# Joining values products with later scores on TensorE, and a retuned order of work, in an attention and mixture-of-experts kernel

## The chip, the cores and the metric

The kernel runs on one core of one Trainium2 chip. The metric is the device time of one execution in microseconds (us), the median of several runs; less is better.

## The reference

Attention with two kinds of mask feeds a dense mixture of experts. The shapes are batch 4, 8 heads, sequence 576, head width 64; then 2304 rows of 512, 4 experts, inner width 1024, all in float32.

```python
scores = scale * np.matmul(q, k.transpose(0, 1, 3, 2))
mask_local = (rel >= 0) & (rel < stride)          # heads 0 to 3, stride 32
mask_strided = (rel >= 0) & (pos[None, :] % stride == pos[:, None] % stride)   # heads 4 to 7
scores = np.where(masks[None, :, :, :], scores, -1000000000.0)
attn = softmax(scores)                            # max, exp, sum + 1e-9, divide
x = np.matmul(attn, v)                            # heads side by side: 2304 x 512
...
p = domain_probs / (domain_probs.sum(-1, keepdims=True) + 1e-09)
for e in range(E):
    h = np.maximum(x @ w1[e], 0.0)
    out += p[:, e:e + 1] * (h @ w2[e])
```

## The kernel before, in words

**Attention.** The work is cut into 16 pairs of two heads each, in the order of the batches, and within a batch local, strided, local, strided (`KORD`). `plan_pair(n)` records the steps of pair n: the loads of q, k and v on SP's queue; the scores on TensorE (L627 for local, L616 for strided heads) into the PSUM tag `sc`; the masking out of PSUM on DVE (L641); the maximum (L644), its subtraction (L647), exp on ACT (L651), the sum (L655) and the division (L659); the transposes on TensorE (L706, L722, L739) into `ps`; their copies `pT` (L526, L528); the values product on TensorE (L771, for the first batch's local heads L791) into `ps`; and the copies of the result into `x` as a high and a low part (`xh` L849, `xl` L852) or as it is (`xr`). PSUM has four banks `mo`, two `sc` and two `ps` (`BANKS`).

**Experts.** There are eight units (an expert and half of its inner width). For the first 384 rows each unit takes a plain first product (L969, 48 matmuls of 384 columns) and a plain second one (L985, 36 matmuls of 512 columns), each with operands split into a high and a low part (ACT L884, then VectorE or GpSimd L885). These run from about 18 to 197 us, with the attention of the later pairs between them. The other 1920 rows follow in two parts, by a scheme with fewer block products (L1155, twelve matmuls to a pair of block products), whose operands come back from DRAM (`ring`, `a`, `s`) and whose sums go out through `acc`. The very last product is cut into two halves of 256 columns in `plan_o`; two additions (L1338) and two stores (L1340) follow.

**What sets the order.** `Plan` records every step as an operation with an engine, a duration, the names it reads and writes, and a priority (a due time, corrected by the table `SHIFT`). `walk` plays the engines forward and takes, for each engine that is free, the operation that is ready and due first; on TensorE attention and experts take turns by a credit. The result is a fixed list of instructions for each engine, which the engine runs in order. An operation on TensorE is never split: all its matmuls follow each other. In the first 30 us `fill` puts dummy matmuls of 512 columns (L1526, into a free bank) where TensorE would stand idle; at most `FIRST` of them may stand ahead of the first real work. Whoever waits is held up in its place, and so is all behind it on its engine.

```python
add("PE", 1.05 if kd == "L" else 0.88, pv, ...pT, vst..., oks, zg[0] + 7, oks, cols=1092)
...
nc.vector.tensor_reduce(out=psums, in_=prs, op=ALU.add, axis=AX.X)
nc.vector.tensor_scalar_add(out=psums, in0=psums, scalar1=1e-9)      # L1464
```

## Time and profile before

| | |
|---|---|
| median of 3 runs | 778.45 us (776.25 to 778.79) |
| the profiled execution: its time | 778.49 us |
| its span, first to last instruction | 776.7 us |
| PE, TensorE matmul: busy | 765.5 us, 99% of the span |
| DVE, ACT, POOL: busy | 80%, 50%, 27% of the span |

The page divides the span into shares; a timeline row says when an instruction or a merged group of them began and how long it took, and in brackets how long its engine had stood idle before it and what ended that. Matmuls overlap, so the step between two of them is read from their starts. [...] A matmul in plain float32 is two instructions in the trace for each one in the program, with a weight load each.

### The profile page before, as it was taken

How to read it: one execution, taken by the hardware profiler on the slowest of the kernel's cores; microseconds unless marked ns; L12 is line 12 of the kernel's file. 1: busy time of each engine (PE TensorE's matmuls, PEld its weight loads, DVE VectorE, ACT ScalarE, POOL GpSimd, SP SyncE). 2: the span in 40 equal slices, each digit the busy share in tenths (PEclk: the TensorE clock that was granted, in tenths of full speed). 3: DMA queues.
4: the chain of work that ended last, by engine and by line, in shares of the span. 5: the costliest groups of instructions: out<-in, count | busy, mean ns of one | idle time of the engine just before them, and what ended most of it. 6: DMA issues, size and time to landing. Idle time of an engine off the chain costs nothing.

```text
span 776.7 us, 14119 instructions
## 1 busy us (share of the span) xinstructions
PE 765.5 (99%) x5374; PEld 664.6 (86%) x5377; DVE 620.8 (80%) x1016; ACT 385.6 (50%) x726; POOL 206.4 (27%) x198
## 2 busy tenths in 40 slices
PE   7999999999999999999999999999999999999997
PEld 4788888889989999999999998888888888888886
DVE  6877777798698897889798997758765976599895
ACT  4635544474566375646727654644354344523330
POOL 5412011012131522454373264001000330033250
PEclk9999999999999999999999999999999999999999
DMA  9999999778899798899989838955665697659624
GB/s 321 305 394 380 339 326 353 276 252 327 311 388 343 257 359 288 328 237 350 350 254 275 272 119 221 395 207 220 236 265 198 193 215 288 232 173 247 215 82 162
DMA packets 89630, 212.67 MB, mean 274 GB/s; under 512 B 7071, under 2 KB 33883, under 8 KB 89563
## 3 DMA queue, kind: packets, MB, share of 16 engines
q1 hardware_dynamic: 83659, 201.96, 71.8%
q0 software_dynamic: 5760, 9.70, 7.9%
q8 instruction: 42, 0.69, 0.3%
q10 hardware_dynamic: 144, 0.11, 0.1%
q14 instruction: 25, 0.20, 0.1%
HBM read 138.58 MB, written 73.17 MB: 273 GB/s over the span
## 4 chain that ended last, share of the span: by engine, by line
PE 95%; DVE 2%; DMA 1%; ACT 1%; issue 1%; POOL 0%; DVEq 0%; ACTq 0%
PE mo L1155 26%; PE ps L1155 25%; PE sc L1155 20%; PE mo L985 9%; PE mo L969 9%; PE ps L771 2%; DMA ring<-d27a 1%; PE sc L627 1%; PE ps L739 1%; PE sc L616 1%; PE mo L1526 1%; PE ps L791 0%; ACT q L1207 0%; DVE w2t L885 0%; DVE pmL L641 0%
## 5 line engine op out<-in xcount | busy, mean ns | idle before, releaser
L1155 PE MATMUL sc<-T,ring 128*128 128x448 f32 (+2 forms) x774 | 174.3, 374 | 0.0
L1155 PEld LDWEIGHTS sc<-T,ring 128*128 128x128 f32 x774 | 144.5, 188 | 19.7
L1240 ACT ACTIVATE T<-q 128x512 fp32r<-128x512 f32 (+1 forms) x196 | 112.6, 601 | 69.0 <-PE mo L1155 26.4
L1242 DVE TENSOR_TENSOR T<-q,T 128x512 fp32r<-128x512 f32 (+1 forms) x152 | 104.7, 703 | 15.9 <-ACT T L1240 15.2
L1203 DVE TENSOR_TENSOR q<-ps,v 128x448 f32<-128x448 f32 (+1 forms) x96 | 62.5, 654 | 35.3 <-PE ps L1155 30.9
L1155 PE MATMUL mo<-T,ring 128*128 128x512 f32 (+1 forms) x396 | 90.0, 376 | 0.0
L1207 ACT ACTIVATE q<-q 128x448 f32<-128x448 f32 (+1 forms) x84 | 49.9, 598 | 71.7 <-DVE q L1203 70.8
L1155 PEld LDWEIGHTS mo<-T,ring 128*128 128x128 f32 x396 | 74.3, 188 | 10.3
L1242 POOL TENSOR_TENSOR T<-q,T 128x448 fp32r<-128x448 f32 (+1 forms) x44 | 53.1, 1215 | 91.8 <-ACT T L1240 69.9
L985 PE MATMUL mo<-w2t,hs 128*128 128x512 f32 x288 | 71.2, 397 | 0.0
L1194 ACT ACTIVATE v<-mo 128x448 f32<-128x448 f32 (+1 forms) x96 | 54.5, 567 | 25.7 <-PE mo L1155 25.0
L1352 DVE TENSOR_TENSOR acc<-sc,acc 128x512 f32<-128x512 f32 (+1 forms) x85 | 54.9, 654 | 13.9 <-PE sc L1155 13.1
L1284 POOL TENSOR_TENSOR q<-q,q 128x512 f32<-128x512 f32 (+1 forms) x12 | 15.4, 1284 | 181.5 <-DVE T L1242 164.9
L985 PEld LDWEIGHTS mo<-w2t,hs 128*128 128x128 f32 x288 | 52.7, 188 | 11.0
L1284 DVE TENSOR_TENSOR q<-q,q 128x448 f32<-128x448 f32 (+1 forms) x88 | 58.9, 681 | 2.5 <-POOL T L1242 1.4
L526 ACT ACTIVATE acc<-sc 128x448 f32<-128x448 f32 (+1 forms) x41 | 23.2, 567 | 48.5 <-PE sc L1155 46.9
L969 PE MATMUL mo<-xh,a 128*128 128x384 f32 x192 | 45.7, 341 | 0.0
L1352 DVE TENSOR_TENSOR acc<-mo,acc 128x512 f32<-128x512 f32 (+1 forms) x52 | 34.0, 658 | 14.0 <-PE mo L1155 11.3
L1155 PE MATMUL ps<-T,ring 128*128 128x448 f32 (+1 forms) x180 | 40.8, 375 | 0.5 <-DMA ring<-d27a 0.5
L1155 PEld LDWEIGHTS ps<-T,ring 128*128 128x128 f32 x180 | 33.7, 188 | 5.3 <-DVE acc L1352 0.8
L1155 PE MATMUL ps<-t4h,a 128*128 128x448 f32 (+1 forms) x128 | 35.2, 376 | 0.2 <-DVE q L1203 0.2
L1155 PE MATMUL ps<-t3h,s 128*128 128x448 f32 (+1 forms) x128 | 35.2, 376 | 0.1
(179 smaller groups left out, 1437.6 us busy)
## 6 DMA issues: line engine op xcount, KB each, us to landing
raw<-in_w SPq DMA_DIRECT2D x28, 1024.0 KB, 8.3
qkS<-in_qk_strided SPq DMA_DIRECT2D x16, 329.0 KB, 8.2
vstL<-in_v_local SPq DMA_DIRECT2D x6, 640.0 KB, 9.7
po<-acc POOLq DMA_DIRECT2D x16, 224.0 KB, 7.2
vstS<-in_v_strided SPq DMA_DIRECT2D x8, 384.0 KB, 7.8
a<-d16a SPq DMA_DIRECT2D x6, 512.0 KB, 8.7
ring<-d27a SPq DMA_DIRECT2D x6, 512.0 KB, 6.5
a<-d10a SPq DMA_DIRECT2D x6, 512.0 KB, 4.7
```

What stands on the lines that cost most here:

```text
L526: nc.scalar.activation(out=dst(), in_=src(held[key]), func=AF.Copy)
L771: nc.tensor.matmul(oo[hf][64 * h:64 * h + 64, o:o + w], a, pt[r, x, c0:c0 + w], start=True, stop=True)
L969: nc.tensor.matmul(pt[:, 0:TA], w[:, c % 2, (f % 2) * P:(f % 2) * P + P], (xl if i == 1 else xh)[c], start=j == 0, stop=j == 11)
L985: nc.tensor.matmul(pt, ht[f][:, ts], wt[f][:, cs], start=j == 0, stop=j == 11)
L1155: nc.tensor.matmul(pt, a[i == 2][:, j, f * P:f * P + P], skewed(b[i == 1][j], TH)[:, cs], start=bool(first) and n == 0, stop=True, skip_gr ...
L1194: add("ACT", TH / 1200 + 0.18, lambda: nc.scalar.activation(out=late["u"][i][:, 0:TH], in_=held[key][:, 0:TH], func=AF.Copy), [key, "late2 ...
L1203: add("DVE", DD, lambda: nc.vector.tensor_tensor(out=q(), in0=src(), in1=late["u"][i][:, 0:TH], op=ALU.add), [key, f"u{i}", "late2"], [tok ...
L1207: add("ACT", TH / 1200 + 0.2, lambda: nc.scalar.activation(out=q(), in_=q(), func=AF.Relu), ["late2"], [tok], zs)
L1240: add("ACT", TH / 1200 + 0.17, lambda src=src, hi=hi: nc.scalar.activation(out=hi(), in_=src(), func=AF.Copy), [tok, "late2"], [f"T{i}h{j} ...
L1242: add("VP", vp, lambda e, src=src, hi=hi, lo=lo: engine(e).tensor_tensor(out=lo(), in0=src(), in1=hi().bitcast(F32), op=ALU.subtract), [to ...
L1284: add("VP", vp, lambda e, d=d, x=x, y=y: engine(e).tensor_tensor(out=d[0](), in0=x[0](), in1=y[0](), op=ALU.subtract), [x[1], y[1]], [d[1] ...
L1352: add("DVE", DD, lambda av=av, key=key: nc.vector.tensor_tensor(out=av(), in0=held[key][:, 0:TH], in1=av(), op=ALU.add), [key], tok, zd)
```

## The change

From the sixth pair on (pairs 6 to 15, `JOINED`) the scores are no operation of their own: `plan_pair` became a generator that hands its scores to the pair two before it, whose values product and these scores are now one operation on TensorE, with the names and banks of both. After an attention operation the planner keeps to attention while one is ready within 0.2 us (`STAY`). Twelve dummy matmuls of 64 columns (`PAD`) follow the scores of pair 1, at most six dummies precede the first scores (`FIRST`), short gaps get none (`SHORT`). The addition of 1e-9 to the sums of the expert weights takes a tile of that constant (`tiny`) in place of a scalar. The last product is cut into 384 and 128 columns. Some entries of `SHIFT` and two durations are others, so that operations stand in another order on every engine up to about 240 us; the number of matmuls of the computation is the same.

```diff
-    92: -3.6, 95: -12.5, 96: -7.9, 100: -3.6, 101: -23.3, 110: 14, 116: -12.2, ...
+    92: -3.6, 95: -12.5, 96: -7.9, 100: -3.6, 101: -23.3, 110: -1.3, 116: -12.2, 121: -23.9, 122: -23.9, 123: -42.2, 141: 9.3,
...
-    FIRST = 9
+    STAY = 0.2
+    FIRST = 6
+    SHORT = 0.3
...
-                if f + step > s and not forced or not out and n >= self.FIRST:
+                if f + step > s and not forced or last["PE"] is None and n >= self.FIRST:
...
+                elif e == "PE" and s0 > STEADY and last[e] is not None and not last[e].moe and any(
+                        not c[1].moe and c[0] <= s0 + self.STAY for c in cand):
+                    pick = min((c for c in cand if not c[1].moe), key=lambda c: (c[0], c[1].prio, c[1].idx))
...
-                    n, f2 = fill(f, s, o) if tag else (0, f)
+                    n, f2 = fill(f, s, o) if tag and s - f > self.SHORT else (0, f)
...
+    JOINED = range(6, 16)
+    AHEAD = 2
+    PAD = 12
...
+                    for _ in range(PAD if n == 1 else 0):
+                        nc.tensor.matmul(ss[0][:, 6 * W:6 * W + 64], wz[:, 0:P], wz[:, 0:64], start=True, stop=True)
...
+                if n in JOINED:
+                    yield spec
+                    plan.number += 1
+                else:
+                    add("PE", *spec[:4], z + 3, keys, cols=4 * nel)
...
-            add("PE", 1.05 if kd == "L" else 0.88, pv, [f"pT{kd}{x}" for x in range(2)] + [f"vst{kd}{bf}{x}" for x in range(2)], oks, zg[0] + 7, oks,
-                cols=1092)
+            spec = (1.05 if kd == "L" else 0.88, pv, [f"pT{kd}{x}" for x in range(2)] + [f"vst{kd}{bf}{x}" for x in range(2)], oks, oks, 1092)
+            if n + AHEAD in JOINED:
+                other = next(pairs[n + AHEAD])
+                d, both, reads, writes, banks, cols = (x + y for x, y in zip((spec[0], [pv], *spec[2:]), (other[0], [other[1]], *other[2:])))
+                add("PE", d, lambda: [x() for x in both], reads, writes, zg[0] + 7, banks, cols=cols)
+            else:
+                add("PE", *spec[:4], zg[0] + 7, oks, cols=1092)
...
-                for x in range(2):
-                    cs = slice(x * TH // 2, (x + 1) * TH // 2)
+                for x, (c0, c1) in enumerate(((0, 3 * TH // 4), (3 * TH // 4, TH))):
+                    cs = slice(c0, c1)
...
-        nc.vector.tensor_scalar_add(out=psums, in0=psums, scalar1=1e-9)
+        nc.vector.tensor_tensor(out=psums, in0=psums, in1=tiny, op=ALU.add)
...
+        nc.vector.memset(tiny, 1e-9)
```

Three places of the new order follow; line numbers after the change are those of the changed file. The first is TensorE where the fourth quarter of `x` (`xh_245`, `xl_249` before, one more after, as `tiny` takes a number) meets the first product of the first unit. Before:

```order
L969 MATMUL mo<-xl_247,s_80 128x384
L969 MATMUL mo<-xh_243,s_80 128x384
L627 MATMUL sc<-qkL_262 32x63 x24
L791 MATMUL ps<-pTL,vstL_266 64x96 x4
L969 MATMUL mo<-xh_245,a_78 128x384
```

After:

```order
L994 MATMUL mo<-xl_248,s_81 128x384
L994 MATMUL mo<-xh_244,s_81 128x384
L816 MATMUL ps<-pTL,vstL_267 64x96 x4
L1508 MATMUL ps<-ident,pr 60x128
L994 MATMUL mo<-xh_246,a_79 128x384
```

The scores of pair 6 no longer stand here; the small transpose of the expert weights does.

The second is TensorE a unit later, at the values product of pair 4, between a first product and a second one. Before:

```order
L969 MATMUL mo<-xh_244,a_79 128x384
L969 MATMUL mo<-xh_245,a_79 128x384
L771 MATMUL ps<-pTL,vstL_265 64x32 x36
L985 MATMUL mo<-w2t,hs_250 128x512 x2
L985 MATMUL mo<-w2t,hs_254 128x512
```

After:

```order
L994 MATMUL mo<-xh_245,a_79 128x384
L994 MATMUL mo<-xh_246,a_79 128x384
L791 MATMUL ps<-pTL,vstL_266 64x32 x36
L637 MATMUL sc<-qkL_263 32x63 x24
L994 MATMUL mo<-xh_243,s_81 128x384
```

The values product of pair 4 is followed at once by the scores of pair 6, here and in nine more places.

The third is VectorE from the sums of the expert weights to the last low part of the fourth quarter of `x`. Before:

```order
L1463 TENSOR_REDUCE psums<-prs 128x18
L1464 TENSOR_SCALAR psums<-psums 128x18
L1465 RECIPROCAL psums<-psums 128x18
L1466 TENSOR_TENSOR pr<-prs,psums 128x72
L641 TENSOR_TENSOR pmL_269<-sc,both 128x3x63 x2
L885 TENSOR_TENSOR w2t<-raw_226,w2t 128x512 x2
L641 TENSOR_TENSOR pmL_269<-sc,both 128x3x63
L644 TENSOR_REDUCE mx<-pmL_269 128x9
L862 COPY xr_241<-ps 128x6x6x3
L852 TENSOR_TENSOR xl_249<-ps,xh_245 128x6x12x3
L885 TENSOR_TENSOR a_77<-raw_225,a_77 128x512
L852 TENSOR_TENSOR xl_249<-ps,xh_245 128x6x12x3
```

After, from the addition on:

```order
L1490 TENSOR_TENSOR psums<-psums,tiny 128x18
L1491 RECIPROCAL psums<-psums 128x18
L1492 TENSOR_TENSOR pr<-prs,psums 128x72
L536 COPY pTS<-ps 128x6x64
L651 TENSOR_TENSOR pmL_270<-sc,both 128x3x63 x2
L910 TENSOR_TENSOR w2t<-raw_227,w2t 128x512
L651 TENSOR_TENSOR pmL_270<-sc,both 128x3x63
L654 TENSOR_REDUCE mx<-pmL_270 128x9
L877 TENSOR_TENSOR xl_250<-ps,xh_246 128x6x12x3
L887 COPY xr_242<-ps 128x6x6x3
L910 TENSOR_TENSOR a_78<-raw_226,a_78 128x512
L887 COPY xr_240<-ps 128x192
```

One subtraction of a weight went to GpSimd, a copy of transposed scores and one of `xr` came from ACT, and the first low part moved ahead of a copy.

## Rows read from the trace of the kernel before

**Rows 1.** the page: an instruction queue (packets, MB); the chain by engine

```profile
q8 instruction: 42, 0.69, 0.3%
PE 95%; DVE 2%; DMA 1%; ACT 1%; issue 1%; POOL 0%; DVEq 0%; ACTq 0%
```

**Rows 2.** stretches: busy us of PE, PEld, DVE, ACT, POOL; PEclk, DMA share, GB/s

```profile
10.00:20.00 10.00, 7.27 (x147) 5.84 (x150) 9.57 (x26) 6.70 (x15) 7.79 (x11) 1.00 1.03 383
20.00:30.00 10.00, 8.62 (x147) 7.04 (x147) 7.03 (x17) 5.78 (x14) 3.06 (x9) 0.83 1.02 358
40.00:60.00 20.00, 20.00 (x194) 17.40 (x192) 14.47 (x27) 7.67 (x15) 3.20 (x3) 1.00 1.05 395
```

**Rows 3.** PE timeline, start: start us, us, what, [idle before, releaser]

```profile
10.97 0.85 PE L706 MATMUL ps<-ident,pmL 128*128 128x128 f32 x6 [0.99 <-DVE pmL L659]
18.56 0.42 PE L969 MATMUL mo<-xh,a 128*128 128x384 f32 x1
20.98 0.78 PE L771 MATMUL ps<-pTS,vstS 54*64 54x54 f32 x34
23.14 0.45 PE L771 MATMUL ps<-pTS,vstS 54*64 54x54 f32 x14 [1.38 <-issue]
28.32 0.52 PE L969 MATMUL mo<-xh,a 128*128 128x384 f32 x2
36.16 0.44 PE L969 MATMUL mo<-xl,a 128*128 128x384 f32 x1 [0.52 <-DVE xl L852]
```

**Rows 4.** stretches of half a microsecond, columns as in Rows 2

```profile
23.50:24.00 0.50, 0.50 (x7) 0.48 (x3) 0.00 (x0) 0.38 (x2) 0.00 (x0) 0.64 1.00 405
27.00:27.50 0.50, 0.50 (x6) 0.45 (x5) 0.00 (x0) 0.33 (x1) 0.00 (x0) 0.95 1.06 373
```

**Rows 5.** PE timeline around one scores operation that stands alone

```profile
120.08 0.69 PE L969 MATMUL mo<-xh,a 128*128 128x384 f32 x3
120.69 0.53 PE L627 MATMUL sc<-qkL 64*32 64x63 f32 x24
121.16 0.61 PE L969 MATMUL mo<-xh,a 128*128 128x384 f32 x2
```

**Rows 6.** the chain that ended last: one piece of 48 first-product matmuls

```profile
164.45 8.34 PE mo L969 x48
```

**Rows 7.** timeline of DVE and POOL, 28 to 37 us

```profile
28.58 0.69 DVE L885 TENSOR_TENSOR w2t<-raw,w2t 128x512 fp32r<-128x512 f32 x1
29.44 1.10 DVE L1464 TENSOR_SCALAR psums<-psums 128x18 f32<-128x18 f32 x1
34.43 1.21 DVE L885 TENSOR_TENSOR a<-raw,a 128x512 fp32r<-128x512 f32 x1
29.22 1.28 POOL L885 TENSOR_TENSOR w2t<-raw,w2t 128x512 fp32r<-128x512 f32 x1 [2.63 <-issue]
33.95 1.14 POOL L647 TENSOR_TENSOR pmL<-pmL,mx 128x567 f32<-128x567 f32 x1 [3.45 <-DVE mx L644]
```

**Rows 8.** timeline of the start: PEld's first scores, POOL's first split

```profile
4.72 0.62 PEld L627 LDWEIGHTS sc<-qkL 64*32 64x32 f32 x24 [0.84 <-DMA qkL<-in_qk_local]
16.75 1.27 POOL L885 TENSOR_TENSOR a<-raw,a 128x512 fp32r<-128x512 f32 x1 [0.37 <-ACT a L884]
```

**Rows 9.** near 220 us: a stretch, SP's issue, PE's wait

```profile
210.00:212.00 2.00, 2.00 (x12) 1.78 (x10) 2.00 (x4) 0.96 (x2) 0.00 (x0) 1.00 1.03 416
221.71 2.61 SPq L1395 DMA_DIRECT2D ring<-d27a  x2
231.68 2.65 PE L1155 MATMUL ps<-T,ring 128*128 128x448 f32 x12 [0.50 <-DMA ring<-d27a]
```

**Rows 10.** timeline of ACT: four weight splits in a row

```profile
45.71 2.67 ACT L884 ACTIVATE w2t<-raw 128x512 fp32r<-128x512 f32 x4 [0.99 <-PE mo L985]
```

**Rows 11.** timeline of the end: DVE, SP's DMA issues

```profile
772.80 0.76 DVE L1338 TENSOR_TENSOR acc<-sc,acc 128x256 f32<-128x256 f32 x2 [0.74 <-PE sc L1155]
773.26 0.81 SPq L1340 DMA_DIRECT2D out<-acc  x2
```

## The prediction

> **What bounds the kernel now.** I read the chain that ended last first: 95% of it is TensorE [rows 1]. The page of engine shares says the same (99% busy), so time can be won only where TensorE stands idle, runs at the low clock, or spends steps that are not needed. Next I looked at stretches for where that is. From 40 us on a stretch is full and at full clock [rows 2]; the stretch from 20 to 30 us is neither (8.62 us busy, clock 0.83). So the beginning is to be read by itself, and behind it only single waits.

> The timeline of the start shows when expert work begins: at 18.56 us [rows 3]. From there every idle microsecond of TensorE is lost for good, as all that follows is one unbroken queue of matmuls. There are two such losses. The values product of pair 1 begins at 20.98 us, stops after 34 of its 48 instructions, and goes on at 23.14 after 1.38 us idle, which no engine or DMA ended ("issue") [rows 3]. And after this gap the clock falls to half: the stretch from 23.50 us has a mean of 0.64, so it fell at 23.50 + 0.28 x 0.50 = 23.64, and the one from 27.00 has 0.95, so it rose again at 27.05 [rows 4]. [...] Then TensorE waits 0.52 us at 36.16 for the low part of the fourth quarter of `x` from DVE [rows 3]. Far behind, at 231.68, it waits 0.50 us for a weight load [rows 9].

> **The change part by part.**

> *Switches.* Counted in the order of instructions, attention stands in 35 separate places between expert matmuls before and in 32 after. A place costs more than its matmuls. Expert matmuls of 384 columns follow each other every 8.34 / 48 = 0.174 us [rows 6]. Three of them begin at 120.08 [rows 5], so the next could begin at 120.60; the scores begin at 120.69: 0.09 us for going in. Coming out, two expert matmuls take 0.61 us together [rows 5], against 0.52 for two in an unbroken line [rows 3]: 0.09 more. Three places fewer at 0.18 give 0.5 us. None and all of these are the bounds: 0 and -0.5. I take **-0.5**, as the path there is TensorE alone.

> *The gap of 1.38 us.* The change puts 24 instructions (12 dummies with their weight loads) ahead of it, and nothing else that stands there moves. Whatever stops TensorE inside one operation isn't data, since all of that operation reads the same tiles. The page has an instruction queue of 42 packets, 0.69 MB [rows 1], 16 KB each; a packet that comes late is the reading I hold likeliest, and the 24 instructions then move both the place of the stop and the time of the request. The trace cannot say by how much. Bounds: gone (-1.4) or longer by the 0.3 us that the place is reached earlier (12 of 34 matmuls in 0.78 us, [rows 3]). Nearest is the same gap; I take half of it, **-0.7**.

> *The half clock.* It followed a gap, and an earlier gap of 0.99 us at 10.97 [rows 3] was followed by no fall (1.00 from 10 to 20 us, [rows 2]). With half the gap filled by expert matmuls I take the clock as held: **-1.7**, the other bound is 0.

> *The wait at 36 us.* TensorE comes there earlier by 2.4 us from the two terms above, and by 0.7 more since the 48 scores instructions of pair 6 are gone from ahead of it. That is work put off, not saved. DVE stood idle for the same gap, so its chain moves with TensorE; it also loses one weight subtraction (0.69 us, [rows 7]) and gains a copy. The scalar addition took 1.10 us for 18 columns and ended with GpSimd's subtraction (29.22 to 30.50) [rows 7]. Bounds for the wait: gone (-0.5), or longer by the 0.7 us. I take it as it is, **0**.

> Here a row speaks against the new addition. A subtraction with both inputs in SBUF took 1.21 us at 34.43 while GpSimd worked until 35.09, against 0.69 at 28.58 with GpSimd idle [rows 7]: so two-input operations are held up too. [...] I count no gain from this edit; by the row of the old addition it could be 0.8.

> *The start.* The first scores wait for their load until 4.72 us [rows 8], so six dummies in place of eight cost nothing, and the second half of these scores need not let a dummy pass. That is at most 0.6 us earlier for pair 0. Expert work does not follow, since its first weights come from GpSimd at 16.75 + 1.27 = 18.02 [rows 8], behind their load. The twelve dummies of 64 columns fall into the 0.99 us ahead of the transposes at 10.97 [rows 3]; without this cover they would cost, at 64 of 384 columns of an expert step each [rows 6], 12 x 0.174 / 6 = 0.35 us, and at a whole step each 2.1. **0**.

> *The end.* The first addition waits for all of the last product and both take 0.76 us [rows 11]. Now the first has 384 columns, so the first store leaves later; by 0.69 us for 512 columns [rows 7] the 128 more cost at most 0.17. The second store follows the first on SP, 0.81 us for two [rows 11]. Bounds 0 and +0.2; **+0.1**.

> *Moved loads.* On SP a 1 MB weight load now stands behind two other transfers near 210 us, closer to the jam in which DMA is full (1.03, 416 GB/s) and a ring load issued at 221.71 ends TensorE's wait at 231.68 [rows 9]. One megabyte at 416 GB/s is 2.5 us. Bounds: 0.5 less (the wait gone) and 2.5 more. I take **0**, as all these transfers are released by the same work as before.

> The sum is -0.5 - 0.7 - 1.7 + 0.1 = -2.8 us. From the profiled execution, 778.49, which is the median to 0.04 us, it gives 775.7.

> **The rivals.**

> *The gap and the half clock stay.* The 24 instructions move the place of the stop and the request alike. [...] What is left is -0.5 from the switches, -0.5 from the wait at 36 us (TensorE comes 0.7 us of scores earlier, but DVE's chain is shorter by a subtraction) and +0.1: 778.5 - 0.9 = 777.6.

> *The wait at 36 us grows.* If the new addition is held up like the subtraction at 34.43 and TensorE comes early, the wait grows by up to the 0.7 us of the scores: 775.7 + 0.7 = 776.4. [...]

> *Joined operations wait (slower).* A joined operation can't begin before both its parts can, and all expert matmuls stand behind it. ACT splits weights four in a row, 2.67 us [rows 10]; if copies of transposed scores, which the values product reads, come behind such a row, TensorE stands for up to that long. Before, scores or expert work could be put in between. Two such waits in ten joined operations and the gap as before: 777.6 + 2 x 2.67 = 782.9. From one and a half such waits on it is slower than now. Against it: from 40 us on TensorE never waits for such copies now, and DVE and ACT have room (14.47 and 7.67 of 20 us [rows 2]).

> **How the numbers follow.** A measurement of this kernel can tell some 0.3%, 2.3 us, from no change: faster is under 776.1, slower over 780.8. I give the forecast 0.46, the gap that stays 0.29, the longer wait 0.09, the joined waits 0.16. The forecast's own range is 774.0 (gap gone, -0.7 more; wait gone or ring wait gone, -0.5 each) to 776.9 (gap whole, with the clock held, and the ring load later). Four fifths of it lie under 776.1, 0.37; a third of the longer wait, 0.03, and a fifth of the gap that stays, as one term may fall otherwise, 0.06: faster 0.46. Slower are most of the joined waits and a little of a late ring load: 0.15. The rest, 0.39, is the same. For 8 in 10 the range goes from 773.9 to 780.6: it leaves out the joined waits and a twentieth of the forecast.

> **What would show it.** Right: PE has no gap over 0.8 us after 18.56, the granted clock is 1.00 from 10 us to the end, 32 places of attention, and the scores directly behind a values product cost no going in. Wrong: a stop of over 1 us inside an operation near 21 us and a stretch at 0.50 behind it (then the first rival); rows of PE between 40 and 200 us that wait for ACT's copies or for masks (then the last); or a ring wait over 1 us near 230 us.

## The result, and the profile after

The change made the kernel slower: 787.34 us (786.80 to 788.59, 4 runs) against 777.35 us (776.21 to 778.79, 4 runs), a ratio of 1.013 with a 95% interval of 1.011 to 1.0151. The profiled execution took 788.59 us with a span of 786.8 us, 10.1 us more than the span of before.

The chain that ended last is still TensorE's, with 92% in place of 95, and the instruction queue moves as many packets as before [rows 1]:

```profile
q8 instruction: 42, 0.69, 0.3%
...
PE 92%; DMA 1%; ACT 1%; issue 1%; DVE 0%; DVEq 0%
```

**At the start TensorE is ahead.** TensorE's timeline of the changed kernel (columns as in [rows 3]):

```profile
17.75 0.42 PE L994 MATMUL mo<-xh,a 128*128 128x384 f32 x1
...
21.09 0.61 PE L791 MATMUL ps<-pTS,vstS 54*64 54x54 f32 x25 [0.35 <-issue]
...
36.69 0.52 PE L759 MATMUL ps<-ident,pmL 64*128 64x64 f32 x10 [0.62 <-POOL pmL L669]
37.15 1.20 PE L1010 MATMUL mo<-w2t,hs 128*128 128x512 f32 x4
```

Expert work begins 0.8 us earlier, the stop inside the values product of pair 1 is 0.35 us and no longer 1.38, and the second product begins at 37.15 us, where the profiled execution of before began it at 39.23. Not forecast are four waits of 0.37 to 0.72 us for VectorE and GpSimd between 24 and 37 us, one of them in the row of 36.69; with the smaller ones they make 2.5 us, where before had the one of 0.52.

**Then TensorE stops inside scores.** The same view, the three longest stops of the later part:

```profile
103.23 0.92 PE L791 MATMUL ps<-pTS,vstS 54*64 54x54 f32 x48
103.97 0.29 PE L624 MATMUL sc<-qkS 64*64 64x54 f32 x7
105.52 0.81 PE L624 MATMUL sc<-qkS 64*64 64x54 f32 x41 [1.25 <-issue]
...
120.07 0.53 PE L637 MATMUL sc<-qkL 64*32 64x63 f32 x23
121.49 0.24 PE L637 MATMUL sc<-qkL 64*32 64x63 f32 x1 [0.89 <-issue]
...
131.91 1.36 PE L791 MATMUL ps<-pTL,vstL 63*64 63x32 f32 x72
133.20 0.48 PE L637 MATMUL sc<-qkL 64*32 64x63 f32 x33
136.08 0.46 PE L637 MATMUL sc<-qkL 64*32 64x63 f32 x15 [2.40 <-issue]
136.47 6.78 PE L1010 MATMUL mo<-w2t,hs 128*128 128x512 f32 x17
```

They make 1.25 + 0.89 + 2.40 = 4.54 us, all three within one operation that had already begun, none ended by an engine or a DMA ("issue"). Two lie in joined operations (48 and 72 values matmuls, each with 48 scores behind them), the middle one in scores that the planner had put right behind 12 transposes. The row of 136.47 is a sign of what followed: 17 matmuls in 6.78 us, 0.40 us each, where 36 of them took 8.39 us at 37.22, 0.23 us each. The stretches (columns as in [rows 2]):

```profile
100.00:120.00 20.00, 18.75 (x362) 15.72 (x355) 13.83 (x28) 8.18 (x19) 4.91 (x4) 1.00 0.96 336
120.00:140.00 20.00, 16.70 (x306) 14.20 (x301) 13.81 (x25) 8.65 (x19) 3.08 (x3) 0.88 0.72 257
136.10:142.00 5.90, 5.90 (x28) 4.57 (x28) 3.17 (x6) 0.00 (x0) 0.00 (x0) 0.50 0.27 110
```

Before, a stretch like these was full and at full clock [rows 2]. Now they lack 1.25 and 3.30 us, and for 5.9 us behind the last stop the granted clock is 0.50, with 1.00 as full speed, and the matmuls of 512 columns in them begin 427 ns apart (median of 12), where those from 37 to 47 us begin 227 ns apart. Taken as half of the 5.9 us, that costs an estimated 3.0 us.

**And from 200 us on, where TensorE hardly waits, matmuls are a little longer.** Groups of TensorE's instructions by line and shape (busy us, mean ns of one | idle before), first of before, then of after; all have 512 columns:

```profile
L1155 PE MATMUL ps<-t3h,s 128*128 128x512 f32 x64 | 18.4, 389 | 0.0
L1155 PE MATMUL ps<-t2h,s 128*128 128x512 f32 x64 | 18.4, 389 | 0.0
```

```profile
L1180 PE MATMUL sc<-T,ring 128*128 128x512 f32 x378 | 90.9, 389 | 0.0
...
L1180 PE MATMUL ps<-t3h,s 128*128 128x512 f32 x64 | 18.9, 396 | 0.0
L1180 PE MATMUL ps<-b11h,a 128*128 128x512 f32 x64 | 18.8, 396 | 0.0
L1180 PE MATMUL ps<-t4h,a 128*128 128x512 f32 x64 | 18.8, 395 | 0.0
L1180 PE MATMUL mo<-b21h,a 128*128 128x512 f32 x64 | 18.8, 395 | 0.0
L1180 PE MATMUL ps<-t2h,s 128*128 128x512 f32 x64 | 18.4, 389 | 0.0
```

389 ns became 395 or 396 in the products whose streamed operand is `b11`, `b21`, `t3` or `t4`. Counted by the starts of matmuls behind 200 us, 532 of 2,694 steps are longer by 5 to 11 ns than the usual step of their width (227 ns for 512 columns, 201 for 448), 490 of them in these four products; before, 8 of 2,674. Smaller differences add to them: from the first matmul of this part, which has the same 2,694 matmuls in the same order in both kernels, to the last it is 579.9 us in place of 575.1, 4.8 us more.

Set against before, profile to profile: expert work begins 0.8 us earlier. The 2,388 matmuls from there to the first one of the later scheme take 184.9 us in place of 178.8, 6.1 more: stops 1.25 + 0.89 + 2.40 + 0.35 - 1.38 = +3.5, half clock 3.0 - 1.7 = +1.3, the other waits before 37 us 2.5 - 0.5 = +2.0, which leaves -0.7 for the places saved. The rest takes 4.8 more. Together that is the 10.1 us. One plain fact is needed for the rest: of 25 executions of the kernel before that were timed beside later runs, four had a mean clock of 0.997 (the profiled one 0.998) and took 778.3 to 780.1 us, the other 21 had 0.999 or 1.000 and took 775.8 to 778.0.

### The profile page after: what moved, and what is told of

Its sections match the earlier page's. It is cut to its first block, busy times and chain, and to the rows that moved or that the text cites. A ratio compares the mean times of both kernels' runs of the same rounds, so it can differ in the third digit from the quotient of the medians.

```text
span 786.8 us, 14164 instructions
## 1 busy us (share of the span) xinstructions
PE 770.9 (98%) x5385; PEld 666.3 (85%) x5389; DVE 620.3 (79%) x1016; ACT 385.4 (49%) x725; POOL 207.3 (26%) x200
## 4 chain that ended last, share of the span: by engine, by line
PE 92%; DMA 1%; ACT 1%; issue 1%; DVE 0%; DVEq 0%
PE mo L1180 26%; PE ps L1180 26%; PE sc L1180 20%; PE mo L1010 9%; PE mo L994 8%; PE ps L791 2%; DMA ring<-d27a 1%; PE sc L637 1%; PE ps L759 1%; PE sc L624 1%; ACT q L1232 0%; ACT T L1265 0%; ACT v L1219 0%; DVE q L1309 0%; DVE acc L1364 0%
## 5 line engine op out<-in xcount | busy, mean ns | idle before, releaser
L1010 PEld LDWEIGHTS mo<-w2t,hs 128*128 128x128 f32 x288 | 54.8, 194 | 12.3 <-issue 0.2
```

What stands on the lines that cost most here:

```text
L1010: nc.tensor.matmul(pt, ht[f][:, ts], wt[f][:, cs], start=j == 0, stop=j == 11)
```

## The experiments

### Without the new tile

```diff
-    tiny = const.tile([P, NTT], F32, name="tiny")
...
-        nc.vector.tensor_tensor(out=psums, in0=psums, in1=tiny, op=ALU.add)
+        nc.vector.tensor_scalar_add(out=psums, in0=psums, scalar1=1e-9)
...
-        nc.vector.memset(tiny, 1e-9)
```

> The changed kernel without its new constant tile of 18 numbers per partition (the sum is made with a scalar 1e-9 again); TensorE's order is the changed kernel's to the instruction. Address theory: the tile moved every later tile by 72 bytes, and that is what made some 530 matmul steps after 200 us about 10 ns longer; they go back to their old length and the time falls by about 5 us, to 782 us; the three stops inside joined operations (1.25, 0.89 and 2.40 us) and the half clock after 135 us stay. Rival (the slower steps come from the new order of the work, or from the transfers beside it): no change, 787 us.

783.11 us (782.17 to 784.10), ratio 1.0078 (1.0063 to 1.0093); before 776.89. The long steps are gone (8 of 2,687), the three stops stand where they stood: 1.15, 0.94 and 2.40 us. One thing missed: in this profiled execution the clock held through the same stop of 2.40 us:

```profile
134.05 0.48 PE L637 MATMUL sc<-qkL 64*32 64x63 f32 x33
136.94 0.34 PE L637 MATMUL sc<-qkL 64*32 64x63 f32 x15 [2.40 <-issue]
```

```profile
137.00:142.00 5.00, 5.00 (x45) 3.86 (x44) 3.54 (x7) 0.00 (x0) 0.00 (x0) 1.00 0.51 202
```

So a stop of that length may be followed by a fall of the clock, and need not be. The place of the stops can be counted in this trace, by TensorE's matmuls, weight loads and semaphore instructions: its five "issue" stops (13.02, 22.00, 106.31, 122.34 and 136.94 us) come at instructions 450, 706, 3,265, 3,778 and 4,289, so they are 256, 2,559, 513 and 511 apart, multiples of 256 to within one.

### The new tile alone, in the kernel before

```diff
-    warm = const.tile([P, 8], F32, name="warm")
+    warm = const.tile([P, 8], F32, name="warm"); tiny = const.tile([P, NTT], F32, name="tiny")
...
-        nc.vector.memset(wz, 0.0)
+        nc.vector.memset(wz, 0.0); nc.vector.memset(tiny, 1e-9)
```

> The kernel before with the new tile alone, placed and filled as in the changed kernel and read by nobody; TensorE's order is the old one. Address theory: some 500 matmul steps become about 10 ns longer, 783 us in place of 778.4. Rival (order or transfers): no change, 778.4 us.

780.85 us (780.29 to 780.98), ratio 1.0048 (1.0033 to 1.0063): +4.0 us, with 535 long steps, 497 of them in the same four products. Nobody reads this tile. That it alone costs 4 us is shown; the rival has fallen.

### Without the padding

```diff
-                    for _ in range(PAD if n == 1 else 0):
+                    for _ in range(0):
```

> The changed kernel without its 12 padding matmuls (24 instructions of TensorE); all else, the order too, is the same. Block theory (TensorE waits at every 256th instruction until the next 16,384 bytes of its program are there): each stop after the padding moves 12 matmuls later: the one at 105.5 us from the 8th to the 20th matmul of its scores, the one at 136 us (now 33 scores in) to 45 scores in and to about 2.0 us, and the one at 121.5 us falls among expert matmuls, where it is under 0.3 us. Rival (the stops belong to the place: a bank or an operand that the scores wait for): each stop stays at the same matmul with the same length.

786.83 us, one run. TensorE's timeline around the three places:

```profile
104.59 0.51 PE L624 MATMUL sc<-qkS 64*64 64x54 f32 x19
106.21 0.68 PE L624 MATMUL sc<-qkS 64*64 64x54 f32 x29 [1.11 <-issue]
...
120.64 0.53 PE L637 MATMUL sc<-qkL 64*32 64x63 f32 x24
121.10 0.98 PE L994 MATMUL mo<-xh,a 128*128 128x384 f32 x4
...
132.67 0.69 PE L637 MATMUL sc<-qkL 64*32 64x63 f32 x45
135.59 0.30 PE L637 MATMUL sc<-qkL 64*32 64x63 f32 x3 [2.24 <-issue]
```

The first stop now comes after 19 scores matmuls where it came after 7, the last after 45 where it came after 33: 12 matmuls later each, as expected, and the last is 2.24 us; behind it the granted clock is 0.50 from 137.0 to 140.3 us. The scores at 120.64 are no longer stopped, and no expert matmul behind them waits 0.25 us. With data, a bank or a semaphore as cause the stops could not have moved by the number of matmuls taken out far ahead. That they belong to a place in the instruction stream is shown.

### Nothing joined, and no new tile

```diff
-    JOINED = range(6, 16)
+    JOINED = ()
```

The tile is taken out as in the first run.

> The changed kernel with no operation joined (the set of joined pairs is empty, so values products and scores are planned apart again) and without the new tile; padding, six dummies, the rule of the first stretch and the last product stay. Block theory: bursts of 24 to 48 small matmuls with expert matmuls on either side leave time to bring the next 16,384 bytes, so no stop inside scores is over 0.5 us after 40 us, the clock stays at 1.0 from 6 us on, and with the address theory for the tile the time is 775 to 777 us. Rival (the stops come with the new places and the new loads, not with the joining): stops of 1 to 2 us and a stretch of half clock remain, and the time is 781 us or more.

778.34 us (777.43 to 780.21, 10 runs), ratio 1.0022 (1.0012 to 1.0032): 4.8 us less than the joined order without the tile, and still 1.45 us more than before (776.89). The clock held in the profiled execution. One stop stayed, where the planner had set a values product right behind scores, so that 120 small matmuls stand together without being one operation:

```profile
132.36 0.72 PE L637 MATMUL sc<-qkL 64*32 64x63 f32 x48
133.01 0.89 PE L791 MATMUL ps<-pTL,vstL 63*64 63x32 f32 x45
134.84 0.71 PE L791 MATMUL ps<-pTL,vstL 63*64 63x32 f32 x27 [0.94 <-issue]
```

So it is not the joining as such but where the boundary falls. Nor is a burst of 120 enough: the kernel before has two, with the scores first, and runs through both. One of them:

```profile
73.13 0.72 PE L627 MATMUL sc<-qkL 64*32 64x63 f32 x48
73.78 1.36 PE L771 MATMUL ps<-pTL,vstL 63*64 63x32 f32 x72
```

The expected 775 to 777 us was missed by this stop and by two at the start that had not been priced (0.62 us at 21.41, "issue", and 0.72 us at 29.83 for DVE).

### Joined, with the boundaries moved by half a block

```diff
-        for _ in range(n):
-            nc.tensor.matmul(t, wz[:, 0:P], wz, start=True, stop=True)
+        for _ in range(4 * n):
+            nc.tensor.matmul(t[:, 0:P], wz[:, 0:P], wz[:, 0:P], start=True, stop=True)
...
-                    for _ in range(PAD if n == 1 else 0):
+                    for _ in range(PAD + 10 if n == 1 else 0):
```

The tile is out here too.

> The changed kernel without the new tile (as in the first run of these), all operations joined as they were, but with 64 more small matmuls ahead of the first expert product: each dummy of 512 columns is four of 128, and ten paddings are added. The order after that is the same, so only the place of the 256-instruction boundaries moves, by 64 matmuls, half a block. Block theory: the stops at 106.3, 122.3 and 136.9 us go, and with them the half clock; the shortest blocks, and so the only places for a stop over 0.5 us, are now those that end near 102.6 us (a block that TensorE runs through in 3.5 us) and 80.3 us (4.4 us); the time falls from 783.1 to between 780 and 782 us. Rival (a joined operation itself waits, for copies or banks): the three stops stay at 106, 122 and 137 us with 1.2, 0.9 and 2.4 us, 783 to 784 us.

779.56 us (777.65 to 782.76, 5 runs), ratio 1.0043 (1.0024 to 1.0062), a little under the range. The joined operations run through:

```profile
82.51 0.99 PE L637 MATMUL sc<-qkL 64*32 64x63 f32 x48
...
107.45 0.88 PE L624 MATMUL sc<-qkS 64*64 64x54 f32 x48
...
132.81 1.36 PE L791 MATMUL ps<-pTL,vstL 63*64 63x32 f32 x72
134.10 0.72 PE L637 MATMUL sc<-qkL 64*32 64x63 f32 x48
```

From 40 to 200 us no wait of 0.25 us is left, so the three stops are shown to be the boundary's. Of the two places named, the first (83 us here, where all is some 2.5 us later) cost 0.26 us, seen only in the 48 scores at 82.51, which take 0.99 us in place of 0.72, and the second nothing: a block that TensorE runs through in 3.5 us need not end in a stop. The gain was partly given back at the start, where expert work began at 21.13 us:

```profile
13.16 0.88 PE L726 MATMUL ps<-ident,pmL 128*128 128x128 f32 x6 [2.58 <-POOL pmS L657]
...
21.13 0.42 PE L994 MATMUL mo<-xh,a 128*128 128x384 f32 x1
```

The profile puts the 2.58 us down to GpSimd, but the same count of instructions is reached there at which the run without the tile stood still until 13.02 us ("issue", 0.86 us) with 64 more matmuls of the computation done. The first boundary was passed at 12.72 us in the changed kernel ("issue", 0.86 us), at 13.02 without the tile and at 13.16 here, with or without the filler ahead of it, so the filler pushed work behind it. Behind this stop the granted clock is 0.50 from 14.6 to 17.9 us, also ahead of the expert work.

### Nothing joined, with the boundaries moved

The fourth kernel with the dummies split in the same way, nine paddings, and the last product in halves again.

> The fourth run (nothing joined, no new tile) with the boundaries moved by 51 matmuls in the same way, to where no block is run through in under 5 us, and with the last product in two halves of 256 columns again. Block theory: the 0.9 us stop at 134.8 us and the 0.6 us stop at 21.4 us go, and 0.2 us comes back at the end: 776.5 to 777.2 us in place of 778.3, level with the kernel before or 0.3 us under it. Rival (the stop at 134.8 us is one of the new order): 778 us, the stop where it was.

778.41 us (777.55 to 780.84, 11 runs), ratio 1.0027 (1.0017 to 1.0037). The stop at 134.8 us went (TensorE is busy for all of 40 to 160 us), but expert work began at 20.55 us in place of 17.81, for the reason just told. So the stop was the boundary's. But the boundaries made new stops, 1.88 us at 27.15 (put down to DVE, but 512 instructions behind the first one, two blocks) and 1.12 at 35.06, 257 instructions behind that:

```profile
35.06 0.67 PE L637 MATMUL sc<-qkL 64*32 64x63 f32 x43 [1.12 <-issue]
```

The expected time was missed by the later start and these two. TensorE ran through the blocks that end there in some 6 and 7 us, so the 5 us of the expectation are no safe length.

### Two other sizes of the tile

Against the run with the tile alone (the second size has 24 in place of 16):

```diff
-tiny = const.tile([P, NTT], F32, name="tiny")
+tiny = const.tile([P, 16], F32, name="tiny")
```

> The kernel before with a tile of 16 numbers per partition (64 bytes) in place of the 18 (72 bytes) of the second run. If what counts is where later tiles begin within 64 bytes, the steps after 200 us are as short as before and the time is that of the kernel before. If any shift of the later tiles costs (their places against each other are the same, but the whole is moved), 4 us more again, 780.9 us.

> The same with 24 numbers per partition (96 bytes). Within 64 bytes the later tiles are moved by 32. If a place within 32 bytes is what counts, no change from the kernel before; if within 64 bytes, some of the steps after 200 us are longer, 778 to 781 us.

782.12 us (ratio 1.007, 1.0052 to 1.0089) and 781.92 us (1.0068, 1.005 to 1.0086), before 776.41; 647 and 504 long steps. Neither is spared, so a place within 32 or 64 bytes is not what counts. In the built program 72 bytes take 96, so the 72 and 96 byte tiles move the weights by the same; they have about as many long steps (535 and 504), at +4.0 and +5.5 us on two chips.

### The tile behind the weights

```diff
-    wq = {n: (t[:, 0], t[:, 1]) for n, t in wt.items()}
+    wq = {n: (t[:, 0], t[:, 1]) for n, t in wt.items()}; tiny = big.tile([P, NTT], F32, name="tiny")
...
```

> The kernel before with the 72-byte tile of the second run, but taken after the four weight tiles (a11, a12, a22, s3) of that memory side and ahead of all the rest, so that these four stay where they were and everything after them on that side moves by 72 bytes. In the second run the long steps were those of the four products whose weights had been moved against the streamed operand (a11 with b11, a12 with b21, s3 with t3, a22 with t4; t1, b22 and t2 have their weights beside them on the other side, which did not move). Theory (the distance between a product's weights and its streamed operand is what counts): no long steps, the time of the kernel before within 0.5 us. Rival (any tile that moves later tiles costs): some 500 long steps, 4 us more.

778.53 us (777.83 to 779.57, 10 runs), ratio 1.0019 (1.0007 to 1.003). The four products are short again but for a rest in `b11`. 107 steps are long, 33 of them in `b11` and 61 in the products of `T` with `ring`, and the part behind 197 us takes 1.0 us more than before:

```profile
L1155 PE MATMUL ps<-b11h,a 128*128 128x512 f32 x64 | 18.6, 392 | 0.0
L1155 PE MATMUL ps<-t3h,s 128*128 128x512 f32 x64 | 18.4, 389 | 0.0
```

Most of the 4 us hangs on where these four weights stand. The 1.7 us left over are not within the 0.5 us expected; the 1.0 us of steps is a part, the rest is open.

### The streamed operands moved: a run that moved nothing, and one that did

> The kernel before with 72 bytes taken on the other memory side, ahead of the streamed operands (b11 to t4) and the weights s1, s2 and s4 beside them; nobody writes or reads them, and a11, a12, a22 and s3 stay where they were. By the distance theory this is the second run over again from the other end: the products of b11, b21, t3 and t4 have about 530 long steps, those of t1, b22 and t2 few, and the time is 4 us over the kernel before. Rival (it is the place of the weights itself that counts): no long steps and no change.

776.41 us (775.72 to 782.59, 10 runs), ratio 0.9999 (0.9978 to 1.002), 3 long steps. The built program has every operand at its old address, so this run tests nothing of the theory: it is the kernel before once more. The other run moved them:

```diff
-        p.tile([P, 16], F32, name="skew1")
+        p.tile([P, 40], F32, name="skew1")
```

> The run before it that was to move the streamed operands moved nothing: tiles on that side are placed up from the foot of their pool, and the pool grew downwards by just the new tile. Here an unused tile behind them (the last but the small buffers) is 96 bytes larger, so that in the built program b11 to t4 and s1, s2 and s4 begin 96 bytes lower (b11 at 153,408 in place of 153,504) and a11, a12, a22 and s3 stay (a11 at 4,768; with the new tile of the change, 4,864). Distance theory: a11 with b11, a12 with b21, s3 with t3 and a22 with t4 stand to each other exactly as in the changed kernel, so these four products have some 530 long steps of about 10 ns and the time is 4 us over the kernel before. Rival (the place of the weights alone counts): these four stay short; if anything changes it is t1, b22 and t2, whose weights moved, by up to 3 us.

781.94 us (781.43 to 782.24, 4 runs), ratio 1.006 (1.0043 to 1.0077), before 777.13: +4.8 us, with 524 long steps, 484 of them in the same four products:

```profile
L1155 PE MATMUL ps<-t3h,s 128*128 128x512 f32 x64 | 18.9, 396 | 0.0
L1155 PE MATMUL ps<-b11h,a 128*128 128x512 f32 x64 | 18.8, 396 | 0.0
L1155 PE MATMUL mo<-b22h,s 128*128 128x512 f32 x64 | 18.5, 391 | 0.0
L1155 PE MATMUL ps<-t2h,s 128*128 128x512 f32 x64 | 18.4, 389 | 0.0
```

The weights of `t3` and `b11` did not move here and the steps are those of the changed kernel to the nanosecond; the weights of `t2` and `b22` moved, together with their streams, and those steps are 389 and 391, again as in the changed kernel (389 and 389 before; why `b22` gains 2 ns there, though its operands keep their distance, is open). That the distance between a product's weights and its streamed operand sets its step is shown for the distances tried: that of before is short, 64 and 96 bytes more are long.

### The padding alone, in the kernel before

```diff
+                    for _ in range(12 if n == 1 else 0):
+                        nc.tensor.matmul(ss[0][:, 6 * W:6 * W + 64], wz[:, 0:P], wz[:, 0:64], start=True, stop=True)
```

> The kernel before with nothing but the 12 padding matmuls of the change, put into the same scores, so that every later 256-instruction boundary comes 12 matmuls earlier in its program. Block theory: of the old order's blocks those that end near 34.8 and 78.5 us are then the shortest (3.3 and 4.3 us, where its own shortest is 5.5), so TensorE stops there for 0.5 to 1.5 us, and the time rises by 1 to 3 us, the 0.5 us of the padding itself among it. Rival (only joined operations stop): no stop over 0.5 us after 30 us, at most 0.5 us more.

778.21 us (777.51 to 781.21, 10 runs), ratio 1.0019 (1.0004 to 1.0034): +1.4 us.

```profile
77.53 0.92 PE L773 MATMUL ps<-pTS,vstS 54*64 54x54 f32 x48
78.38 0.52 PE L629 MATMUL sc<-qkL 64*32 64x63 f32 x20
79.89 0.30 PE L629 MATMUL sc<-qkL 64*32 64x63 f32 x4 [0.99 <-issue]
```

The old order, nothing joined, stops for 0.99 us inside the scores that begin at 78.38 us, at one of the two places named; at 34.8 us, behind a block of 3.2 us, it did not. Twenty-four instructions put in ahead of 12 us made a stop at 79, so the rival has fallen. The stop in the values product of pair 1 is still there, longer than before, and the clock fell behind it (0.50 from 23.7 to 27.0 us):

```profile
23.10 0.61 PE L773 MATMUL ps<-pTS,vstS 54*64 54x54 f32 x26 [1.59 <-issue]
```

## Why the prediction was wrong

*The bound* ("time can be won only where TensorE stands idle, runs at the low clock, or spends steps that are not needed") was right, and it is also where the time was lost.

*The half clock, -1.7, and the gap, -0.7.* The -1.7 was the author's estimate, half of the 3.41 us from 23.64 to 27.05 us in which the granted clock was 0.50; no run shows it as the change's gain, and 3.0 us of the same kind came behind 136 us. In the profiled execution of the changed kernel the stop was 0.35 us and the clock held, but that this is the change's doing isn't shown. The same order without the tile stopped for 0.90 us; the padding alone left 1.59 us and the half clock. In the old order the profiled executions with the clock held (the runs with another tile or another place) had from nothing to 0.81 us there. So the stop varies by the execution in either order, and the reasoning by 24 instructions has no support. As terms of the sum both failed, because they belonged to the one profiled execution. In that of the unmoved kernel, with a stop of 0.77 us, the old order began its second product at 37.42 us, 1.8 us before the profiled execution that was read and 0.3 behind the changed kernel:

```profile
37.42 1.44 PE L985 MATMUL mo<-w2t,hs 128*128 128x512 f32 x5
```

So most of these 2.4 us, of the forecast 2.8, was not there to be won in most executions. The text said that the profiled time was the median; the lowest of the three runs, 776.25 us, was 2.2 us under it and was the sign to heed.

*The switches, -0.5.* The mechanism holds and is small, as predicted: in the run with nothing joined, 48 values matmuls or 48 scores add 0.945 us each between expert matmuls, and joined they added 1.645, so 0.245 us is won where two places become one, 0.7 us for three. The stops took back over six times that.

*From 40 us on, "one unbroken queue of matmuls".* This is the step that failed most. It took the old stream's freedom from stops as a property of the place. It was one of the arrangement: moving the instruction count by 24 (12 matmuls with their weight loads) broke it without any other edit. The reading was on the page: a packet of the instruction queue that comes late, with 24 instructions moving the place of the stop. It was applied to the one gap that could be seen, not to the ten new bursts of up to 240 instructions. In place of the free stretch the runs showed three stops at block boundaries, 4.5 us together, with 3.0 us of half clock behind the last.

*The last rival* (joined operations wait, 782.9) had the side and two waits in ten operations right, and the mechanism wrong: no row of the changed kernel shows TensorE waiting for ACT's copies behind 40 us. Its "from one and a half such waits on it is slower than now" is also off: 0.9 us, a third of such a wait, makes up the difference to 778.5.

*The new addition, "no gain from this edit".* The reading was right: beside a GpSimd subtraction (26.08 to 28.61 us in the changed kernel) the addition takes 1.01 us with the tile (first row) and 1.00 with the scalar (second, the run without the tile):

```profile
26.38 1.01 DVE L1490 TENSOR_TENSOR psums<-psums,tiny 128x18 f32<-128x18 f32 x1
27.33 1.00 DVE L1490 TENSOR_SCALAR psums<-psums 128x18 f32<-128x18 f32 x1
```

But the constant it reads needed a tile, and the tile's place cost 4.0 to 4.2 us by itself (+4.0 with it alone, -4.2 without it). The prediction never costed the tile; that is the second step that failed.

*The end, +0.1.* Mis-sized: the last product's matmuls take 1.2 + 0.8 us busy against 1.6 us in halves, since the six of 128 columns follow each other every 0.11 us, not in a third of the time of 384; about 0.2 us, with none of it won back behind.

*The start, 0.* Expert work was not to begin earlier, since GpSimd's split of its first weights ends at 18.02 us. But this split moved with the start, from 16.75 to 15.79 us, and expert work began at 17.75 in place of 18.56.

*The moved loads, 0,* hold: the ring wait near 230 us is 0.2 us (0.50 before, [rows 9]). *The wait at 36 us, 0:* this one wait is gone, but the 2.5 us of waits between 24 and 37 us stand in its place (0.62 us at 36.69 for GpSimd among them), 2.0 us more. The bound was 0.7.

Summed up against the old kernel beside the first four runs, 776.89 us: the tile 4.23 us (787.34 less 783.11), the joining with its order, its stops and the half clock 4.77 (783.11 less 778.34), the rest of the change 1.45, together the 10.45 us to 787.34. Of the 1.45 only the one stop of 0.94 us and the waits of the start are seen in the trace; no run took them apart. No version tried beats the old kernel.

Left open: what makes a packet late, why the same stop is followed by half clock in one execution and not in another, and why a shift of 64 or 96 bytes lengthens steps. The trace only bears on the first: the packet ahead of the 2.40 us stop began at 133.65 us, some 5 us after TensorE had passed the boundary before, in a stretch in which DMA was full (a share of 0.99 from 128.4 to 133.6 us). Fewer transfers at that time were not tried.

## What to carry to other kernels

Where TensorE bounds and small matmuls stand between large ones, count instructions: here TensorE stopped for 0.9 to 2.4 us inside runs of small matmuls, at places 256 instructions or a multiple apart to within one. Twenty-four instructions fewer near 10 us moved two of these stops by 12 matmuls (1.11 and 2.24 us then), and twenty-four more made one of 0.99 us in the old order, so an order without stops was not kept by an edit that added a few. A new small tile can move the weights of a product against its streamed operand (by 64 or 96 bytes here): it cost 4.0 us ahead of the weights and 1.7 behind them, so the mean step of each product is to be compared before and after. A stop or a half clock seen in one execution is a gain only if other executions have it too.

## What the runs showed that was not expected

The stops end 1.36 to 1.52 us after the last byte of an instruction packet has come (packets of 0.9 to 1.0 us that ended at 104.08, 120.06 and 134.56 us in the changed kernel, at 78.53 with the padding alone), so at these four some 1.4 us of the stop lie behind the packet's arrival. At the stops of 12.72 and 21.09 us in the changed kernel it was 1.49 and 1.27 us, and at that of 23.14 us before, 0.89.

A distance of 64 or 96 bytes more between two operands lengthens a matmul of 512 columns in four products from a mean of 389 ns to one of 394 to 397, which no wait or idle row shows: it is to be seen in mean durations alone.
